# Layer 1's entry in a streaming two-layer decode kernel: ticks on VectorE, a loop entered without the last kept scores, and two early copies

## The chip, the cores and the metric

The kernel runs on one core of one Trainium2 chip. Its time is the device time of one launch in microseconds; three runs of the kernel before were timed, and their median is used. Only a difference of more than about 0.2% (5.1 us) is counted as faster or slower.

## The reference

Two rows `x` (B = 2, D = 576) go twice through an attention block A and a mixer block B, with the same caches and weights both times:

```
x = x + A(layernorm(x)); x = x + B(layernorm(x))      # layer 0
x = x + A(layernorm(x)); x = x + B(layernorm(x))      # layer 1

A: q = x @ wq                      # 32 heads of 128, one query row per batch
   scores = q . k_cache * 128**-0.5 over 16384 keys
   o = softmax(scores) @ v_cache
   return o @ wo
B: h = gelu(layernorm(x) @ w1); shifts of h @ w2 -> hs
   x1 = x + hs
   return x1 + gelu(layernorm(x1) @ w3) @ w4
```

`k_cache` and `v_cache` are (2, 32, 16384, 128) in bf16: 64 pairs of batch and head, 4096 KB of K and 4096 KB of V each. Both layers read all of both, so that nearly all bytes of the run are cache tiles.

## The kernel before

**Tiles and slots.** One K tile or one V tile is 128 partitions x 32768 B (`TILE`). On-chip memory has six slots of that size, numbered 0 to 5, and a small area `AUX` ahead of them, which holds the three buffers `kt[0..2]` for transposed chunks of K. A head's K tile holds 128 blocks of 128 keys; it is treated as two halves of 64 blocks (`BP`). In each half the first 32 blocks (`PB`) go to TensorE and the other 32 to VectorE.

**One head in the loop** (`attention`, the loop over `s`). TensorE takes its blocks in eight chunks of eight blocks (`CH`): `transposes` writes a chunk to a PSUM bank `tps`, `evacuate` copies it on ScalarE to a `kt` buffer (line 1257), and `scores` multiplies it with the query column `q_col` (line 1272) into the bank `sps[s % 3]`. VectorE handles the other blocks in four calls of `dots`, at chunks 0, 2, 4 and 6: a product with the broadcast query `qb` (TENSOR_TENSOR, line 1302) and a sum (TENSOR_REDUCE, line 1306). These four cover blocks 32 to 47, 48 to 63, 96 to 111 and 112 to 127. After the first `dots`' chunk, at `c == LEAD`, VectorE also runs `keep_o(s - 2)` (line 1343: the finished output of an earlier head leaves the PSUM column `ops`), `softmax_max(s - 1)` (lines 1317 and 1319), then the second `dots`, then `q_column(s + 1)` (line 1188). `first_max(s)` (line 1311) closes the head on VectorE. `softmax_exp(s - 1)` on ScalarE and `pv` (line 1362) on TensorE finish the head before. The loop runs over 63 heads, as 21 turns of three, on TensorE, ScalarE and VectorE; the code of GpSimd and SyncE is written out.

**Transfers.** All transfers go through one queue on SyncE, in the order in which they were planned (`Store.plan`). `pump` issues the head of that list as soon as all memory cells of its place have been released in program order; SyncE then waits for the semaphores of the operations that used the place last. Most tiles are one transfer of 4096 KB. Layer 1's first new tiles are cut: the rest of `v61` into three pieces, `k0` into quarters 0, 1, 3, 2 for slot 1, and `k1` into quarters 0, 2, 1, 3 for slot 3. After them come `v0`, `k2`, `v1`, `k3` and so on as whole tiles. Layer 1 takes the heads in the order 63, 61, 62, 0, 1, ...; the K tiles 61 to 63 and the V tiles 62 and 63 are kept from layer 0. So `k0` takes the place of K63 (head s = 0 of layer 1), `k1` that of K61 (s = 1), and `k2` that of K62 (s = 2).

**Signals.** An operation has a target `to`. One with `to="vector"` increments a semaphore that only VectorE waits on; one with `to=None` increments its engine's common semaphore. When another engine has to wait for an operation whose `to` is not that engine, `_stand_in` lets it wait for the next operation of the same engine with `to=None`:

```
x = next(x for x in self.ops[d.eng][d.pos + 1:] if x.to is None and not x.relay)
```

All operations of `dots` have `to="vector"`, `q_column` and `keep_o` have `to="tensor"`. In the loop of the kernel before, the operations of VectorE with `to=None` are the second operation of `softmax_max` (line 1319) and `first_max`. SyncE therefore waits on line 1319 for the first `dots` of a head, and on `first_max` for the second, third and fourth.

**Waits at a loop's entry.** A wait inside a loop has to have the same form in each turn. Where the first turn has a wait that later turns don't have, `_loop` puts it ahead of the loop (`ahead`).

**Layer 1's head s = 0.** Its K tile lies on chip while layer 0 still runs its mixer. `ahead` transposes its chunks early: four chunks stay in the four `tps` banks (`held_over`, "kept chunks"), twelve (`early`) are copied back in place by `lay`. When the query is there, `early_scores` (line 1287) makes the scores of the twelve, VectorE copies part of them (line 1103) and takes `first_max(0)`. Then the four kept chunks are evacuated to `kt` and scored, and the loop begins.

Of the kernel before, what the change touches and what calls it, by code (L numbers as in the profile page):

```python
# [338 lines left out]
class KB:  # L339
# [718 lines left out]
    def attention(self, l):  # L1058
        U, LEAD, NS = self.U, self.LEAD, self.NS
        o = self.order(l)  # L1060
        n = self.PB // self.CH
        pend = []

        def step(s, c):
            self.transposes(l, s, o[s], c)
            pend.append((s, o[s], c, self.chunk))
            self.chunk += 1
            self.evacuate(pend[-1][3])
            if len(pend) > LEAD:
                self.scores(*pend.pop(0))  # L1070

        def rest():
            while pend:
                self.scores(*pend.pop(0))

        if l == 0:
            self.store.claim("kt", 0, self.AUX)
            zero = self.zero[:, 0, 0:1]
            self.pe(lambda pe: pe.matmul(self.mps[:, 448:449], lhsT=self.ident[:, :], rhs=zero, start=True, stop=True,
                                         skip_group_check=True), reads=["ident", "zero"], writes=["ops", "mps"], to="vector").needed = True  # L1080
            self.q_broadcast(0)
            self.landed("k", o[0], True)
            for c in range(2 * n):
                step(0, c)
                if c % n in (0, 2):
                    self.dots(l, 0, o[0], c // n, c % n // 2)
                if c == LEAD:
                    self.q_column(1)
            rest()
            self.q_spread(1)  # L1090
            self.first_max(0)
        else:
            self.lay(0, len(self.laid))
            assert self.made == len(self.early) and len(self.held_over) == self.HOLD
            pend += self.held_over
            self.chunk += len(self.early) + self.HOLD
            w = self.NB - 2 * self.PB
            for i, (h, b, col) in enumerate(self.early):
                self.early_scores(l, o[0], h * self.BP + b, col)
                if i == 1:  # L1100
                    self.q_broadcast(1)
                if i == w // self.CH - 1:
                    self.dv(lambda e: e.tensor_copy(out=self.s_dve[0][:, 0:w], in_=self.mps[:, 2 * self.PB:self.NB]),
                            reads=["mps"], writes=[("s_dve", 0)], to="vector")
                    self.first_max(0)
            self.store.claim("kt", 0, self.AUX)
            for i, x in enumerate(self.held_over):
                if i >= self.NKT:
                    self.scores(*pend.pop(0))
                self.evacuate(x[3])  # L1110
            rest()
        first = self.g.mark()
        for s in range(1, U):
            self.landed("k", o[s], True)
            for c in range(2 * n):
                step(s, c)
                if c == LEAD:
                    self.keep_o(s - 2)
                    self.softmax_max(s - 1)
                if c % n in (0, 2):  # L1120
                    self.dots(l, s, o[s], c // n, c % n // 2)
                if c == LEAD:
                    self.q_column(s + 1)
            self.first_max(s)
            rest()
            self.softmax_exp(s - 1)
            self.q_spread(s + 1)
            self.landed("v", o[s - 1], False)
            for g in range(4):
                self.pv(l, s - 1, o[s - 1], g)  # L1130
        self.g.loop(first, (U - 1) // NS, NS, self.HEAD[l])
        self.touch(ACT.Exp)
        self.ahead(l, self.HOLD)
        self.store.release("kt")
        self.last_head(l, U - 1, o[U - 1])

    def last_head(self, l, s, u):

        U, late = self.U, self.late
        first = next(a + late - v for a, v, n in self.runs(l) if v <= late < v + n)  # L1140
        assert self.order(l)[first] == late and first < s
        i, hg = self.ident[:, :], self.HG
        every = bass.AP(tensor=i.tensor, offset=i.offset, ap=[list(i.ap[0]), [1, hg], [0, hg], [hg, 128 // hg]])
        self.softmax_max(s)
        self.keep_o(s - 1)
        self.dv(lambda e: e.tensor_copy(out=self.every.rearrange("p (j h m) -> p j h m", j=hg, h=hg), in_=every),
                reads=["ident"], writes=["prod", "every"])
        self.shares(0, first)
        self.normed(l, 0, first)
        self.ahead(l, 1)  # L1150
        self.dealt(0, late, self.sps[2], ("sps", 2), self.masked[0], self.oA[:, :], "oA")
        self.lay(l, 1)
        self.ahead(l, 1)
        self.softmax_exp(s)
        self.touch(ACT.Sqrt)
        self.lay(l, 1)
        self.landed("v", u, False)
        for g in range(4):
            self.pv(l, s, u, g)
        self.keep_o(s, None)  # L1160
        n = [sum(c[0] < a for c in self.cuts["wo", l]) for a in (1, 2)] + [len(self.cuts["wo", l])]
        for i in range(n[0]):
            self.heads_projection(l, i)
        self.shares(first, U)
        self.normed(l, first, U)
        for i in range(n[0], n[1]):
            self.heads_projection(l, i)
        self.dealt(late, U, self.sps[0], ("sps", 0), self.masked[1], self.oB[:, :], "oB")
        self.ahead(l, 1)
        self.lay(l, 1)  # L1170
        for i in range(n[1], n[2]):
            self.heads_projection(l, i)
        self.add_rows(self.x, "x", self.sps[1], ("sps", 1))
# [89 lines left out]
        n = self.CH * 256  # L1263
        return self.store.key(k * n, n)

    def scores(self, s, u, c, at):
        k = at % self.NKT
        sp = s % self.NS

        def f(pe):  # L1270
            for j in range(self.CH):
                ins = pe.matmul(self.sps[sp][:, c * self.CH + j:c * self.CH + j + 1], lhsT=self.kt[k][:, j, :],  # L1272
                                rhs=self.q_col[:, sp:sp + 1], start=True, stop=True, skip_group_check=True)
            return ins
        last = c == 2 * self.PB // self.CH - 1
        self.pe(f, reads=[("q_col", sp)] + self.kt_keys(k), writes=[("sps", sp)], sig=("s", c, k, sp),
                to="vector" if last else None)

# [171 lines left out]
```

## Time and profile before

| | |
|---|---|
| median of 3 runs | 2553.53 us (2553.32 to 2553.66) |
| profiled execution, its own time | 2553.28 us |
| its span in the trace | 2551.2 us |
| time outside the span | 2.08 us |
| bytes moved, mean rate over the span | 1093.00 MB, 428 GB/s |
| busy: PE, DVE, ACT, POOL | 1523.6, 1875.7, 1115.2, 164.2 us |

PE is TensorE, DVE is VectorE, ACT is ScalarE, POOL is GpSimd, SP is SyncE; SPq and POOLq are their queues of instructions. All times of the trace count from the span's start. In timelines the columns are start, duration, engine, line, operation, `out<-in`, count, and in brackets the engine's idle time ahead of the row with what ended it. In tables of stretches each engine has its busy time and, in parentheses, its count of instructions; the last three columns are the clock granted to TensorE, the mean busy share of the 16 DMA engines, and the rate in GB/s.

### The profile page before, as it was taken

How to read it: one execution, taken by the hardware profiler on the slowest of the kernel's cores; microseconds unless marked ns; L12 is line 12 of the kernel's file. 1: busy time of each engine (PE TensorE's matmuls, PEld its weight loads, DVE VectorE, ACT ScalarE, POOL GpSimd, SP SyncE). 2: the span in 40 equal slices, each digit the busy share in tenths (PEclk: the TensorE clock that was granted, in tenths of full speed). 3: DMA queues.
4: the chain of work that ended last, by engine and by line, in shares of the span. 5: the costliest groups of instructions: out<-in, count | busy, mean ns of one | idle time of the engine just before them, and what ended most of it. 6: DMA issues, size and time to landing. Idle time of an engine off the chain costs nothing.

```text
span 2551.2 us, 75163 instructions
## 1 busy us (share of the span) xinstructions
PE 1523.6 (60%) x34485; PEld 1435.3 (56%) x34485; DVE 1875.7 (74%) x1794; ACT 1115.2 (44%) x1833; POOL 164.2 (6%) x161
## 2 busy tenths in 40 slices
PE   5555555655565565556677655565565556556556
PEld 4555555555555555555677655555555555555555
DVE  5877776777777677777649877777677777777773
ACT  3444444443444444344355443444344344434442
POOL 0000000000000000000000000000000000000000
PEclk8666666666666666666657666666666666666665
DMA  9999999999999999999999999999999999999999
GB/s 412 428 433 430 433 431 432 432 432 433 431 433 431 433 430 433 430 433 430 422 379 430 430 433 431 433 432 432 432 432 432 431 432 431 433 431 434 430 434 387
DMA packets 46498, 1093.00 MB, mean 428 GB/s; under 512 B 5114, under 2 KB 6780, under 8 KB 11516
## 3 DMA queue, kind: packets, MB, share of 16 engines
q1 hardware_dynamic: 46460, 1092.46, 99.9%
q8 instruction: 28, 0.46, 0.1%
q14 instruction: 10, 0.08, 0.0%
HBM read 1092.44 MB, written 0.00 MB: 428 GB/s over the span
## 4 chain that ended last, share of the span: by engine, by line
DMA 70%; DVE 19%; issue 8%; PE 2%; SPq 0%; ACT 0%; POOLq 0%; DVEq 0%
DMA mem<-in_A_k_cache_dram 64%; DVE prod L1302 9%; DVE s_dve L1306 9%; DMA mem<-in_B_w_dram 2%; DMA mem<-in_A_wo_dram 2%; DMA mem<-in_A_v_cache_dram 2%; PE tps L1242 0%; PE mps L1362 0%; SPq L98 0%; DVE mx L1311 0%; DVE mx L1319 0%; DMA mem<-in_A_wq_dram 0%; DVE q_col L1188 0%; DVE o_acc L1343 0%; DVE mx L1317 0%
## 5 line engine op out<-in xcount | busy, mean ns | idle before, releaser
L1257 ACT ACTIVATE mem<-tps 128x1024 bf16<-128x1024 bf16 x1020 | 958.2, 1035 | 1289.7 <-PE tps L1242 1286.3
L1242 PE MATMUL tps<-ident,mem 128*128 128x128 bf16 x8160 | 813.8, 271 | 708.5 <-POOLq L187 707.9
L1306 DVE TENSOR_REDUCE s_dve<-prod 128x16 f32<-128x2048 bf16 x508 | 1161.4, 2286 | 17.4
L1242 PEld LDWEIGHTS tps<-ident,mem 128*128 128x128 bf16 x8160 | 670.3, 124 | 718.5 <-POOLq L187 717.4
L1302 DVE TENSOR_TENSOR prod<-mem,qb 128x2048 bf16<-128x2048 bf16 x508 | 621.3, 1223 | 541.1 <-POOLq L187 530.4
L1362 PE MATMUL mps<-p,mem 128*128 128x1 bf16 x16384 | 450.4, 165 | 83.3 <-POOLq L187 73.1
L1362 PEld LDWEIGHTS mps<-p,mem 128*128 128x128 bf16 x16384 | 443.0, 102 | 98.2 <-ACT p L1336 97.0
L1272 PE MATMUL sps<-q_col,mem 128*128 128x1 bf16 x8160 | 369.0, 166 | 161.4 <-ACT mem L1257 144.0
L1272 PEld LDWEIGHTS sps<-q_col,mem 128*128 128x128 bf16 x8160 | 320.8, 101 | 217.8 <-ACT mem L1257 211.4
L1322 POOL PARTITION_ALL_REDUCE mx<-mx x128 | 160.3, 1252 | 2334.9 <-DVE mx L1319 2334.9
L1332 ACT ACTIVATE p<-s_dve,mx 128x64 bf16<-128x64 f32 x128 | 44.7, 349 | 15.5
L1201 ACT ACTIVATE qb<-sps 128x128 bf16<-128x128 f32 x129 | 34.1, 264 | 32.7 <-PE sps L1198 32.7
L1198 PE MATMUL sps<-ident,q_col 128*128 128x128 bf16 x129 | 29.8, 231 | 20.2 <-DVE q_col L1188 20.2
L1336 ACT ACTIVATE p<-sps,mx 128x64 bf16<-128x64 f32 x128 | 37.7, 295 | 0.0
L1330 ACT ACTIVATE mx<-mx 128x1 f32<-128x1 f32 x128 | 30.3, 237 | 12.9 <-POOL mx L1322 12.9
L1311 DVE TENSOR_REDUCE mx<-s_dve 128x1 f32<-128x64 f32 x128 | 28.2, 220 | 4.5
L882 PE MATMUL sps<-xn,mem 128*128 128x2 bf16 x544 | 21.4, 173 | 13.8 <-DMA mem<-in_A_wq_dram 7.5
L882 PEld LDWEIGHTS sps<-xn,mem 128*128 128x128 bf16 x544 | 20.0, 119 | 15.3 <-DMA mem<-in_A_wq_dram 8.3
L1317 DVE TENSOR_REDUCE mx<-sps 128x1 f32<-128x64 f32 x128 | 27.4, 214 | 0.7 <-DVEq L259 0.7
L1343 DVE COPY o_acc<-mps 128x1 f32 (+1 forms) x130 | 19.3, 149 | 7.2 <-PE mps L1362 7.2
L1198 PEld LDWEIGHTS sps<-ident,q_col 128*128 128x128 bf16 x129 | 12.6, 98 | 21.1 <-DVE q_col L1188 21.1
L1336 ACT ACTIVATION_READ_ACCUMULATOR p<-sps,mx (+1 forms) x128 | 24.4, 191 | 0.0
(107 smaller groups left out, 228.0 us busy)
## 6 DMA issues: line engine op xcount, KB each, us to landing
mem<-in_A_v_cache_dram SPq DMA_DIRECT2D x125, 4096.0 KB, 45.5
mem<-in_A_k_cache_dram SPq DMA_DIRECT2D x123, 4096.0 KB, 43.2
mem<-in_A_wq_dram SPq DMA_DIRECT2D x8, 1024.0 KB, 11.7
mem<-in_A_k_cache_dram SPq DMA_DIRECT2D x8, 1024.0 KB, 7.5
mem<-in_B_w_dram SPq DMA_DIRECT2D x14, 576.0 KB, 7.2
mem<-in_B_w_dram SPq DMA_DIRECT2D x7, 864.0 KB, 21.3
mem<-in_B_w_dram SPq DMA_DIRECT2D x4, 1152.0 KB, 16.5
mem<-in_A_wo_dram SPq DMA_DIRECT2D x6, 576.0 KB, 8.2
```

Source lines behind the costliest of these rows:

```text
L882: ins = pe.matmul(out[:, m * B:(m + 1) * B], lhsT=buf[:, c:c + 127 * d + 1:d], rhs=self.xn[:, k, :], start=first and m == lo, stop=False, ...
L1198: self.pe(lambda pe: pe.matmul(qps, lhsT=self.wide(self.q_col[:, i:i + 1]), rhs=self.ident[:, :], start=True, stop=True, skip_group_check= ...
L1201: self.act(lambda e: e.activation(out=self.qb[s % self.NS][:, :], in_=qps, func=ACT.Copy), reads=[("qps", i)], writes=[("qb", s % self.NS) ...
L1242: ins = pe.transpose(out[:, j * 128:(j + 1) * 128], buf[:, j * 128:(j + 1) * 128], self.ident[:, :])
L1257: self.act(lambda e: e.activation(out=self.kt[k], in_=self.tps[t][:, :].rearrange("p (i c) -> p i c", i=self.CH), func=ACT.Copy), reads=[( ...
L1272: ins = pe.matmul(self.sps[sp][:, c * self.CH + j:c * self.CH + j + 1], lhsT=self.kt[k][:, j, :], rhs=self.q_col[:, sp:sp + 1], start=True ...
L1302: self.dv(lambda e: e.tensor_tensor(out=prod, in0=buf.rearrange("p (j d) -> p j d", d=128), in1=qbc, op=ALU.mult), reads=[("qb", s % self. ...
L1306: self.dv(lambda e: e.tensor_reduce(out=sd[:, c0:c0 + DB], in_=prod, axis=AX.X, op=ALU.add), reads=["prod"], writes=[("s_dve", s % self.NS ...
L1322: self.pool(lambda e: e.partition_all_reduce(self.mx[:, 3, m:m + 1], self.mx[:, 2, m:m + 1], channels=128, reduce_op=ROP.max), reads=[("mx ...
L1332: self.act(lambda e: e.activation(out=p[:, n:self.NB], in_=self.s_dve[s % self.NS][:, :], func=ACT.Exp, bias=self.mx[:, 4, m:m + 1], scale ...
L1336: self.act(lambda e: e.activation(out=p[:, 0:n], in_=self.sps[i][:, 0:n], func=ACT.Exp, bias=self.mx[:, 4, m:m + 1], scale=self.scale, acc ...
L1362: ins = pe.matmul(self.mps[:, 448:449], lhsT=buf[:, j * 128:(j + 1) * 128], rhs=p[:, col:col + 1], start=(h == 0 and b == 0), stop=(h == 1 ...
```

## The change

Four things change, all in `attention` and `scores`:

- `tick()`: a new one-element copy on VectorE behind `q_column(s + 1)`, in each head of both loops. It has `to=None`, so it becomes the stand-in for the second `dots` of a head.
- In layer 1, the claim of `AUX` moves ahead of the early scores, and two of the four kept chunks are evacuated there, ahead of the query. The third is evacuated behind the second early chunk and `q_broadcast(1)`; the first kept chunk is scored and the fourth evacuated behind the fourth early chunk; the other three are scored behind the twelfth.
- The last kept scores get `to="vector"` (`last=True`).
- The matmul with zeros into the column `ops`, which layer 0 had ahead of its loop, becomes the function `first_o` and is also called ahead of layer 1's loop. It, too, has `to="vector"`.

```
         if l == 0:
             self.store.claim("kt", 0, self.AUX)
-            zero = self.zero[:, 0, 0:1]
-            self.pe(lambda pe: pe.matmul(self.mps[:, 448:449], lhsT=self.ident[:, :], rhs=zero, start=True, stop=True,
-                                         skip_group_check=True), reads=["ident", "zero"], writes=["ops", "mps"], to="vector").needed = True
+            self.first_o()
             self.q_broadcast(0)
...
             self.lay(0, len(self.laid))
             assert self.made == len(self.early) and len(self.held_over) == self.HOLD
-            pend += self.held_over
+            held = self.held_over
             self.chunk += len(self.early) + self.HOLD
+            self.store.claim("kt", 0, self.AUX)
+            for x in held[:2]:
+                self.evacuate(x[3])
             w = self.NB - 2 * self.PB
             for i, (h, b, col) in enumerate(self.early):
                 self.early_scores(l, o[0], h * self.BP + b, col)
                 if i == 1:
                     self.q_broadcast(1)
+                    self.evacuate(held[2][3])
+                if i == 3:
+                    self.scores(*held[0])
+                    self.evacuate(held[3][3])
                 if i == w // self.CH - 1:
                     self.dv(lambda e: e.tensor_copy(out=self.s_dve[0][:, 0:w], in_=self.mps[:, 2 * self.PB:self.NB]),
                             reads=["mps"], writes=[("s_dve", 0)], to="vector")
                     self.first_max(0)
-            self.store.claim("kt", 0, self.AUX)
-            for i, x in enumerate(self.held_over):
-                if i >= self.NKT:
-                    self.scores(*pend.pop(0))
-                self.evacuate(x[3])
-            rest()
+            for x in held[1:]:
+                self.scores(*x, last=x is held[-1])
+            self.first_o()
         first = self.g.mark()
...
                 if c == LEAD:
                     self.q_column(s + 1)
+                    self.tick()
             self.first_max(s)
...
+    def tick(self):
+
+        self.dv(lambda e: e.tensor_copy(out=self.sc[:, 8, 0:1], in_=self.mean_f[:, :]), reads=["mean_f"], writes=["tick"])
+
+    def first_o(self):
+
+        zero = self.zero[:, 0, 0:1]
+        self.pe(lambda pe: pe.matmul(self.mps[:, 448:449], lhsT=self.ident[:, :], rhs=zero, start=True, stop=True,
+                                     skip_group_check=True), reads=["ident", "zero"], writes=["ops", "mps"], to="vector").needed = True
...
-    def scores(self, s, u, c, at):
+    def scores(self, s, u, c, at, last=False):
...
-        last = c == 2 * self.PB // self.CH - 1
+        last = last or c == 2 * self.PB // self.CH - 1
         self.pe(f, reads=[("q_col", sp)] + self.kt_keys(k), writes=[("sps", sp)], sig=("s", c, k, sp),
                 to="vector" if last else None)
```

## The prediction

> **What bounds the kernel now.** I read the page first, then the stretches around the seam between the layers, then the timelines of the engines there.
>
> ```profile
> span 2551.2 us, 75163 instructions
> ...
> DMA  9999999999999999999999999999999999999999
> GB/s 412 428 433 430 433 431 432 432 432 433 431 433 431 433 430 433 430 433 430 422 379 430 430 433 431 433 432 432 432 432 432 431 432 431 433 431 434 430 434 387
> ```
>
> The DMA engines are busy all along, and nearly every slice of 63.8 us moves 430 to 434 GB/s. I take 432 as the full rate; a 4096 KB tile (4.19 MB) then takes 9.7 us, a quarter 2.4. An edit that moves no bytes can only win where the rate sags: the first slice, the slices of 422 and 379 at the seam, and the last. The table in stretches of 5 us shows where the seam loses:
>
> ```profile
> 1325.00:1330.00 5.00, 3.17 (x85) 2.52 (x82) 4.97 (x4) 4.00 (x10) 0.00 (x0) 0.98 1.01 395
> 1330.00:1335.00 5.00, 5.00 (x121) 5.00 (x119) 4.90 (x5) 1.56 (x2) 0.00 (x0) 0.50 0.25 105
> 1335.00:1340.00 5.00, 4.38 (x90) 4.05 (x87) 4.90 (x7) 5.00 (x7) 1.25 (x1) 0.84 0.88 328
> 1340.00:1345.00 5.00, 3.69 (x123) 3.43 (x124) 4.96 (x4) 2.00 (x7) 0.00 (x0) 0.85 1.17 496
> 1345.00:1350.00 5.00, 5.00 (x82) 5.00 (x80) 4.90 (x5) 3.35 (x4) 0.00 (x0) 0.50 0.99 423
> 1350.00:1355.00 5.00, 3.43 (x77) 3.00 (x74) 4.90 (x7) 4.67 (x7) 1.25 (x1) 0.97 0.87 334
> 1355.00:1360.00 5.00, 3.38 (x125) 3.38 (x126) 4.97 (x4) 0.77 (x5) 0.00 (x0) 0.71 0.97 416
> ```
>
> The last column sums to 2497, or 12.5 MB in 35 us; at 432 GB/s they take 28.9 us, so the seam loses 6.1 us here: most in one hole around 1330 to 1336, about 1 us in a second at 1350. VectorE (third column) meanwhile is busy without a pause. What SyncE was waiting for:
>
> ```profile
> 1323.42 0.33 SPq L98 DMA_DIRECT2D mem<-in_A_k_cache_dram  x1
> 1326.62 0.33 SPq L98 DMA_DIRECT2D mem<-in_A_k_cache_dram  x1
> ...
> 1334.52 0.80 SPq L98 DMA_DIRECT2D mem<-in_A_k_cache_dram  x2
> 1335.37 0.43 SPq L98 DMA_DIRECT2D mem<-in_A_v_cache_dram  x1
> ...
> 1349.28 0.33 SPq L98 DMA_DIRECT2D mem<-in_A_k_cache_dram  x1
> 1349.65 0.43 SPq L98 DMA_DIRECT2D mem<-in_A_v_cache_dram  x1
> ```
>
> These are k1's quarters 0 and 2 (released by TensorE), its quarters 1 and 3 together, v0, k2 and v1. Quarters 1 and 3 and k2 wait for VectorE:
>
> ```profile
> 1315.17 0.23 DVE L1103 COPY s_dve<-mps 128x64 f32<-128x64 f32 x1 [1.64 <-PE mps L1287]
> 1315.43 0.22 DVE L1311 TENSOR_REDUCE mx<-s_dve 128x1 f32<-128x64 f32 x1
> 1319.69 1.23 DVE L1302 TENSOR_TENSOR prod<-mem,qb 128x2048 bf16<-128x2048 bf16 x1 [4.04 <-PE sps L1272]
> ...
> 1323.15 0.15 DVE L1343 COPY o_acc<-mps 128x1 f32 x1
> 1323.22 0.21 DVE L1317 TENSOR_REDUCE mx<-sps 128x1 f32<-128x64 f32 x1
> ...
> 1324.79 2.29 DVE L1306 TENSOR_REDUCE s_dve<-prod 128x16 f32<-128x2048 bf16 x1
> 1327.00 0.15 DVE L1188 COPY q_col<-q_f 128x1 bf16 x1
> 1327.12 1.22 DVE L1302 TENSOR_TENSOR prod<-mem,qb 128x2048 bf16<-128x2048 bf16 x1
> 1328.37 2.29 DVE L1306 TENSOR_REDUCE s_dve<-prod 128x16 f32<-128x2048 bf16 x1
> 1330.69 1.22 DVE L1302 TENSOR_TENSOR prod<-mem,qb 128x2048 bf16<-128x2048 bf16 x1
> ...
> 1334.27 0.22 DVE L1311 TENSOR_REDUCE mx<-s_dve 128x1 f32<-128x64 f32 x1
> ...
> 1348.99 0.22 DVE L1311 TENSOR_REDUCE mx<-s_dve 128x1 f32<-128x64 f32 x1
> ```
>
> VectorE is done with `first_max(0)` at 1315.65 and stands still until 1319.69, 4.04 us, held by TensorE's line 1272, the kept scores. From there it runs heads s = 1 and 2 at 14.7 us each (1334.27 to 1348.99). `first_max(1)` ends at 1334.49 and the two quarters go at 1334.52; `first_max(2)` ends at 1349.21 and k2 goes at 1349.28.
>
> **Entering the loop early.** The kept scores and what they wait for:
>
> ```profile
> 1313.91 0.28 ACT L1201 ACTIVATE qb<-sps 128x128 bf16<-128x128 f32 x1 [7.35 <-PE sps L1198]
> 1314.09 2.85 ACT L1257 ACTIVATE mem<-tps 128x1024 bf16<-128x1024 bf16 x3
> 1317.96 1.03 ACT L1257 ACTIVATE mem<-tps 128x1024 bf16<-128x1024 bf16 x1 [1.02 <-PE sps L1272]
> ...
> 1313.67 1.47 PE L1287 MATMUL mps<-q_col,mem 128*128 128x1 bf16 x48
> ...
> 1315.85 0.33 PE L1272 MATMUL sps<-q_col,mem 128*128 128x1 bf16 x7
> 1317.74 0.62 PE L1272 MATMUL sps<-q_col,mem 128*128 128x1 bf16 x17 [1.56 <-issue]
> 1319.04 0.37 PE L1272 MATMUL sps<-q_col,mem 128*128 128x1 bf16 x8 [0.69 <-ACT mem L1257]
> ...
> 1334.90 0.40 PE L1272 MATMUL sps<-q_col,mem 128*128 128x1 bf16 x8
> ```
>
> With its target on VectorE, the last kept scores' signal has the form of every later turn's, so the wait moves from ahead of the loop to `softmax_max(0)`, behind the first `dots`. `first_o` does the same for `keep_o`. The first `dots` needs only `qb(1)` (ready at 1314.19), the tile K61, which is there, and VectorE's turn. That turn is a little later: eight matmuls of the first kept chunk now stand ahead of the copy of line 1103, at 1.47 / 48 = 0.03 us each 0.25 us, so `first_max(0)` ends at 1315.9. To enter the loop VectorE needs between 0.03 us (back to back) and 0.28 us (TensorE's end at 1319.41 to VectorE's start at 1319.69); I take 0.2, as part of that 0.28 may be the signal. The first product starts at 1316.1 instead of 1319.69: 3.6 us earlier (3.5 to 3.75).
>
> It now waits inside the loop, behind the first `dots`, at 1316.1 + 3.46 = 1319.6, with the rest of the head queued behind. TensorE is there in time: the early copies take the two ScalarE pieces of about 1 us off the end, and the 0.69 us wait for the fourth evacuation goes. TensorE's 1.56 us standstill after 104 matmuls (96 early, one broadcast, seven kept) is tied to no wait; I leave it at the same count. Behind it, from 1317.74, are 26 matmuls of 0.03 us, so TensorE is through at 1318.6 instead of 1319.41. Bounds: 1317.1 without the standstill, and 1319.4 if nothing were won. Either is ahead of 1319.6; a doubled standstill would cost VectorE about 0.6 us. TensorE's own chain moves up by 0.8, and k1's quarters 0 and 2 and v0 with it, v0 since it goes on line 1272 of head s = 2 (ended at 1335.30 before, 1334.5 now). The early chunks' quarters of k0 slip by 0.25 to 1.8 us, which the queue covers: the rate holds until 1330, over 10 us on.
>
> **The ticks.** The row of line 1188 shows what a one-element copy costs at this place: between the sum that begins at 1324.79 and the next product at 1327.12 lie 2.33 us, without such a copy (1328.37 to 1330.69) 2.32. So 0.01 us at the least, 0.15 (its busy time) at the most; nothing can be gained, since VectorE runs in order. I take the 0.07 from `keep_o` to the next small operation (1323.15 to 1323.22). The two ticks of heads 1 and 2 take 0.14 us off the lead. What the tick brings: k1's quarter 1 waits for the second `dots` at about 1323.7 instead of `first_max(1)`, and goes right behind quarter 2 at about 1326. Its 2.4 us then fill the first hole's beginning.
>
> **The other ticks**, 124 of them, lie beside transfers:
>
> ```profile
> L1302 DVE TENSOR_TENSOR prod<-mem,qb 128x2048 bf16<-128x2048 bf16 x186 | 227.5, 1223 | 218.7 <-POOLq L187 217.1
> ```
>
> Over 46 heads of layer 1 VectorE waits 217.1 us for tiles to land, 4.7 us a head. A tick costs nothing as long as the head's work stays 4.7 us under its transfers. At the layers' ends tiles are freed with the queue still full, so nothing is counted there. `first_o` is one matmul of 0.03 us.
>
> **The sum, along the transfers.** The old stock runs out at about 1331.2 as before (105 GB/s over 1330 to 1335 are 0.53 MB, 1.2 us at the full rate). Quarter 1 takes it to 1333.6. `first_max(1)` ends 3.5 us earlier, at 1331.0; quarter 3 follows at once. How long until it moves bytes? Before, an issue at 1334.52 gave 328 GB/s over 1335 to 1340, 3.8 us' worth, so it counted from 1336.2, 1.7 us later. So quarter 3 counts from 1333.6 to 1336.0, and v0, issued at 1334.5, from 1336.2 to 1345.9. k2 goes when `first_max(2)` ends, 1349.28 - 3.6 + 0.14 = 1345.8, and counts from 1347.5. Before it counted from 1349.28 + 1.7 = 1351.0 (two quarters and v0 lasted until 1350.8). So the first hole closes, a new one of about 1.6 us opens in front of k2, and everything from k2 on, a continuous stream to the end, moves up by 3.5 us. Of 6.1 us lost, 2.6 remain. Behind k2 each head gives 19.4 us of transfers for 14.7 of VectorE's work, so no third hole opens. The profiled execution's 2553.28 (span 2551.2 plus 2.08) becomes 2549.8; the median lies 0.25 above the profiled time, so the forecast is 2550.0, by its own bounds 2549.4 to 2550.6.
>
> **Rivals.** *The wait stays.* If any other operand of the loop's first turn still holds VectorE until TensorE's kept scores are through, it enters at 1318.6 + 0.28 = 1318.9, and the lead is 0.8 - 0.14 = 0.7: 2552.8. The tick alone then only shifts the hole from before quarter 1 to before k2. For it: the 4.04 us are put down to the releaser that came last, and a second one may stand just behind. Against: the copy, `qb(1)` and K61 are all there by 1316.
>
> *More is won.* If k2 were released by something earlier than `first_max(2)`, up to the whole 6.1 us would come back: 2547.4. Against: k2 is one transfer for a whole tile, and VectorE reads the tile's last blocks just ahead of `first_max(2)`.
>
> *Slower: the ticks are on the path.* If VectorE set the pace of each head, 126 ticks at 0.146 us (line 1188's kind) would cost 18.4 us, less 3.5 won: 2568.4; at 0.07 each, 8.8 - 3.5, 2558.8. The page's chain that ended last and its table of issues bear on it:
>
> ```profile
> DMA 70%; DVE 19%; issue 8%; PE 2%; SPq 0%; ACT 0%; POOLq 0%; DVEq 0%
> ...
> mem<-in_A_k_cache_dram SPq DMA_DIRECT2D x123, 4096.0 KB, 43.2
> ```
>
> For it: VectorE has 19% of that chain. Against: a K tile takes 43.2 us from issue to landing where 9.7 would do, so tiles queue at the transfers and not at VectorE; the rival decides only from 19.4 us of work a head, and there are 14.7. [...]
>
> **How the numbers follow.** The forecast has 0.72, the wait that stays 0.12, more won 0.08, slower 0.08. A difference of 0.2% is 5.1 us, about what a measurement of this kernel can tell from no change; 3.5 us is 0.14%. So same has 0.72 + 0.12 = 0.84, faster 0.08, slower 0.08. The range holds the forecast with 0.4 us more on its fast side, and the wait that stays: 2549.0 to 2553.2, which leaves out 0.16.
>
> **What would show it.** In the changed profile the first product of layer 1 (line 1302) should start near 1316.1 with next to no idle time; `first_max(1)` near 1330.8 and `first_max(2)` near 1345.6; one quarter of k1 should go near 1326, another near 1331. The stretch 1330 to 1335 should be near full rate, and a smaller dip should stand at 1346 to 1348. I am wrong if VectorE still shows a wait for line 1272 ahead of the loop, if it stops behind the first `dots` for TensorE, or if heads in the steady part no longer wait for line 187.

## The result: 2550.47 us, a good 3 us less

| | median | lowest to highest | runs | ratio to before, 95% interval |
|---|---|---|---|---|
| before | 2553.74 | 2552.93 to 2555.32 | 22 | |
| changed | 2550.47 | 2548.54 to 2552.22 | 22 | 0.9986 [0.998, 0.9992] |

In two further sets of runs the changed kernel had medians of 2549.92 and 2549.50 us (11 runs each) beside 2553.78 and 2553.73 before. So it is 3.3 to 4.2 us faster, clear of no difference, yet under 0.2%. The forecast was 2550.0.

The page of the changed kernel, the same lines as were shown of before:

```profile
span 2549.0 us, 75293 instructions
...
DMA  9999999999999999999999999999999999999999
GB/s 413 427 435 429 435 429 435 429 434 430 433 431 431 432 431 433 430 433 430 423 403 424 431 433 431 432 432 431 432 431 433 430 433 430 433 430 433 430 433 381
```

The clear change is in the slices at the seam: 422, 379 and 430 became 423, 403 and 424. In this profiled run layer 0 happened to end 1.2 us later. Times at the seam are therefore compared below as times **behind the query**, the start of the cast that makes layer 1's first `q_col` (line 910): 1312.86 before, 1314.07 here. VectorE's timeline, first of before and then of the changed kernel (start, duration, engine, line, operation):

```profile
1312.86 0.16 DVE L910 CAST q_col<-sps 128x1 bf16<-128x1 f32 x1 [8.92 <-PE sps L882]
```

```profile
1314.07 0.16 DVE L910 CAST q_col<-sps 128x1 bf16<-128x1 f32 x1 [8.93 <-PE sps L882]
...
1316.60 0.23 DVE L1108 COPY s_dve<-mps 128x64 f32<-128x64 f32 x1 [1.85 <-PE mps L1300]
1316.86 0.22 DVE L1324 TENSOR_REDUCE mx<-s_dve 128x1 f32<-128x64 f32 x1
1317.10 1.22 DVE L1315 TENSOR_TENSOR prod<-mem,qb 128x2048 bf16<-128x2048 bf16 x1
...
1322.21 2.29 DVE L1319 TENSOR_REDUCE s_dve<-prod 128x16 f32<-128x2048 bf16 x1
1324.41 0.15 DVE L1201 COPY q_col<-q_f 128x1 bf16 x1
1324.47 0.14 DVE L1142 COPY sc<-mean_f 128x1 f32<-128x1 f32 x1
1324.53 1.22 DVE L1315 TENSOR_TENSOR prod<-mem,qb 128x2048 bf16<-128x2048 bf16 x1
...
1331.68 0.22 DVE L1324 TENSOR_REDUCE mx<-s_dve 128x1 f32<-128x64 f32 x1
...
1346.40 0.22 DVE L1324 TENSOR_REDUCE mx<-s_dve 128x1 f32<-128x64 f32 x1
```

The 4.04 us of standstill ahead of the first product are gone: it starts 0.02 us behind `first_max(0)`, 3.03 us behind the query instead of 6.83. The lead of 3.80 us is still whole at `first_max(2)`, 32.33 us behind the query instead of 36.13. SyncE's issues of the changed kernel (start, duration of issuing, destination and source, count):

```profile
1323.76 0.33 SPq L98 DMA_DIRECT2D mem<-in_A_k_cache_dram  x1
...
1327.02 0.80 SPq L98 DMA_DIRECT2D mem<-in_A_k_cache_dram  x2
...
1331.93 0.33 SPq L98 DMA_DIRECT2D mem<-in_A_k_cache_dram  x1
...
1335.78 0.33 SPq L98 DMA_DIRECT2D mem<-in_A_v_cache_dram  x1
...
1346.70 0.33 SPq L98 DMA_DIRECT2D mem<-in_A_k_cache_dram  x1
```

k1's quarter 1 now goes together with quarter 2 (1327.02), quarter 3 alone behind `first_max(1)`, and k2 at 1346.70, 32.63 us behind the query instead of 36.42. The stretches of 5 us (the last column is the rate):

```profile
1325.00:1330.00 5.00, 3.42 (x86) 3.03 (x84) 4.90 (x4) 4.40 (x10) 0.00 (x0) 0.84 1.01 408
1330.00:1335.00 5.00, 5.00 (x133) 5.00 (x131) 4.93 (x4) 1.11 (x2) 0.00 (x0) 0.50 1.03 403
1335.00:1340.00 5.00, 5.00 (x90) 5.00 (x88) 4.93 (x9) 4.91 (x6) 1.25 (x1) 0.62 1.03 413
1340.00:1345.00 5.00, 3.38 (x115) 3.06 (x113) 4.90 (x4) 2.64 (x8) 0.00 (x0) 0.72 1.01 429
1345.00:1350.00 5.00, 5.00 (x102) 5.00 (x99) 4.93 (x5) 2.86 (x4) 0.00 (x0) 0.60 0.97 377
1350.00:1355.00 5.00, 3.58 (x77) 2.78 (x74) 4.93 (x9) 4.88 (x7) 1.25 (x1) 1.00 0.98 413
1355.00:1360.00 5.00, 4.26 (x136) 4.12 (x136) 4.90 (x4) 0.68 (x5) 0.00 (x0) 0.59 1.02 436
```

The hole of 105 and 328 GB/s is gone; a dip to 377 is left in front of k2. The seven rates sum to 2879, where before they summed to 2497. Reckoned as in the prediction (35 us less sum x 5 / 432), these 35 us lose 1.7 us instead of 6.1. This **loss at the seam** is one measure of the experiments below, beside their medians. It counts packets in fixed stretches, so it has a scatter of its own: 1.4 to 1.7 us in three profiles of the changed kernel.

A second measure is the tiles themselves. From some 128 us behind the query on, VectorE waits once in each head for its K tile to land. The products behind the second of these waits and behind the last, first of before and then of the changed kernel:

```profile
1460.96 1.23 DVE L1302 TENSOR_TENSOR prod<-mem,qb 128x2048 bf16<-128x2048 bf16 x1 [4.63 <-POOLq L187]
...
2490.56 1.23 DVE L1302 TENSOR_TENSOR prod<-mem,qb 128x2048 bf16<-128x2048 bf16 x1 [4.63 <-POOLq L187]
```

```profile
1458.81 1.22 DVE L1315 TENSOR_TENSOR prod<-mem,qb 128x2048 bf16<-128x2048 bf16 x1 [4.62 <-POOLq L187]
...
2488.38 1.23 DVE L1315 TENSOR_TENSOR prod<-mem,qb 128x2048 bf16<-128x2048 bf16 x1 [4.61 <-POOLq L187]
```

That is 148.10 and 1177.70 us behind the query before, and 144.74 and 1174.31 here: the tiles land 3.4 us earlier, at both ends of the stream. This **lead of the tiles** is 1.0 us less than the fall of the loss at the seam, 6.1 - 1.7 = 4.4.

### The profile page after: what moved, and what is told of

The parts are those of the page before. It is cut to its first block, busy times and chain, and to the rows that moved or that the text cites. A ratio compares the mean times of both kernels' runs of the same rounds, so it can differ in the third digit from the quotient of the medians.

```text
span 2549.0 us, 75293 instructions
## 1 busy us (share of the span) xinstructions
PE 1523.7 (60%) x34486; PEld 1434.2 (56%) x34486; DVE 1875.6 (74%) x1920; ACT 1114.2 (44%) x1833; POOL 164.1 (6%) x161
## 4 chain that ended last, share of the span: by engine, by line
DMA 70%; DVE 20%; issue 8%; PE 1%; SPq 0%; POOLq 0%; DVEq 0%; ACT 0%
DMA mem<-in_A_k_cache_dram 64%; DVE s_dve L1319 9%; DVE prod L1315 9%; DMA mem<-in_B_w_dram 2%; DMA mem<-in_A_wo_dram 2%; DMA mem<-in_A_v_cache_dram 1%; DVE mx L1324 0%; SPq L98 0%; DVE mx L1332 0%; DMA mem<-in_A_wq_dram 0%; DVE q_col L1201 0%; DVE o_acc L1356 0%; DVE mx L1330 0%; PE tps L1255 0%; PE sps L882 0%
## 5 line engine op out<-in xcount | busy, mean ns | idle before, releaser
L1345 ACT ACTIVATION_READ_ACCUMULATOR p<-s_dve,mx (+1 forms) x128 | 23.8, 186 | 0.0
```

Of the source, the lines that this page charges most:

```text
L1345: self.act(lambda e: e.activation(out=p[:, n:self.NB], in_=self.s_dve[s % self.NS][:, :], func=ACT.Exp, bias=self.mx[:, 4, m:m + 1], scale ...
```

## The experiments

The theory: k2's issue waits for `first_max(2)`, and VectorE's earlier entry moves that. Two rivals: the ticks carry the gain, as they fill the first hole; or the early copies do, as they free TensorE. Each run stands beside the kernel before of its own set (2553.88 in the first four, 2553.78 in the next four, 2553.73 in the last three).

| run | first product behind the query | k2's issue behind the query | loss at the seam | lead of the tiles, second wait and last | median of 11 | to before, ratio interval |
|---|---|---|---|---|---|---|
| before | 6.83 | 36.42 | 6.1 | | | |
| changed (first profile) | 3.03 | 32.63 | 1.7 | 3.4, 3.4 | 2550.47 (22 runs) | -3.3, [0.998, 0.9992] |
| entry, no ticks | 3.03 | 32.63 | 2.2 | 3.7, 3.2 | 2550.81 | -3.1, [0.9979, 0.9998] |
| ticks alone | 6.98 | 36.58 | 5.3 | 0.5, 0.5 | 2552.65 | -1.2, [0.9987, 1.0005] |
| late copies | 2.82 | 32.78 | 2.5 | 2.5, 2.4 | 2551.33 | -2.6, [0.9981, 0.9999] |
| wait kept | 6.17 | 35.77 | 4.6 | 1.4, 1.3 | 2551.84 | -2.0, [0.9983, 1.0001] |
| changed, second set | 3.03 | 32.62 | 1.4 | 3.5, 3.5 | 2549.92 | -3.9, [0.9977, 0.9995] |
| twelve ticks | 3.03 | 33.93 | 2.8 | 3.1, 3.1 | 2550.13 | -3.7, [0.9977, 0.9995] |
| k2 cut | 3.03 | in quarters | 1.2 | 4.5, 3.8 | 2549.45 | -4.3, [0.9973, 0.9991] |
| k2 cut, no ticks | 3.03 | in quarters | 2.5 | 3.3, 3.3 | 2550.87 | -2.9, [0.9979, 0.9997] |
| k2 cut, third set | 3.04 | in quarters | 0.8 | 5.1, 5.0 | 2549.26 | -4.5, [0.9975, 0.9993] |
| v0 and k2 cut | 3.04 | in quarters | 0.8 | 4.9, 4.7 | 2548.91 | -4.8, [0.9973, 0.9991] |
| changed, third set | 3.04 | 32.64 | 1.5 | 4.3, 4.1 | 2549.50 | -4.2, [0.9974, 0.9992] |

In the nine profiles with k2 in one piece, the tile of the second wait lands 111.0 to 112.8 us behind k2's issue, while the issue itself lies anywhere from 32.6 to 36.6 us behind the query. So the stream follows k2's issue, as the theory has it. The three profiles of the changed kernel have k2's issue at the same distance and differ by 0.9 us in the lead of the tiles, so a difference of less than about 1 us between two single profiles shows nothing by itself. In two runs (entry without ticks, k2 cut in the second set) the stream lost 0.6 us at one head in the middle of layer 1; why isn't known.

**The entry without the ticks.**

```
                 if c == LEAD:
                     self.q_column(s + 1)
-                    self.tick()
```

> The changed kernel without its ticks. Theory (VectorE's earlier entry carries the gain, since k2 waits for first_max(2)): the first product of layer 1 still starts about 3.0 us behind the query (the cast of q_col) instead of 6.8, and first_max(2) about 32.3 us behind it; quarter 1 of k1 goes with quarter 3 at first_max(1), so that a hole of about 1.8 us comes back ahead of it and the one in front of k2 goes; the time is that of the changed kernel, 2550.5 us (2550.0 to 2551.1). Rival (the ticks carry it by filling the first hole): the gain is gone, 2553.7 us.

Median 2550.81. SyncE's issues and the stretch with the hole:

```profile
1330.84 2.29 SPq L98 DMA_DIRECT2D mem<-in_A_k_cache_dram  x2
```

```profile
1330.00:1335.00 5.00, 5.00 (x101) 5.00 (x99) 4.90 (x8) 2.47 (x3) 0.26 (x1) 0.50 0.85 305
```

Quarters 1 and 3 go together again, at `first_max(1)`, and a hole is back in that stretch (305 GB/s, 1.5 us' worth). Most of the gain stays: the loss is 2.2 us, the tiles land 3.7 and later 3.2 us earlier, and k2 goes at the same distance from the query. The rival in which the ticks carry the gain has fallen.

**The ticks alone**: the kernel before, with the line left out above and the function `tick` added.

> The kernel before with the ticks alone. Theory: quarter 1 of k1 goes right behind quarter 2, but first_max(2) stands where it stood, 36.1 us behind the query, so the hole only moves from in front of quarter 1 to in front of k2; 2553.7 us (2553.2 to 2554.2). Rival (the ticks carry the gain): 2550.5 to 2551 us. Rival (ticks are on the path in each head): 2559 us or more.

Median 2552.65, between the theory's 2553.7 and the rival's 2551, and outside the range given; its interval still holds no difference. VectorE's entry and k2's issue:

```profile
1320.07 1.23 DVE L1307 TENSOR_TENSOR prod<-mem,qb 128x2048 bf16<-128x2048 bf16 x1 [4.19 <-PE sps L1277]
```

```profile
1349.67 0.33 SPq L98 DMA_DIRECT2D mem<-in_A_k_cache_dram  x1
```

The query of this run was at 1313.09, so VectorE still stands still until 6.98 us behind it, and k2 goes at 36.58, 0.16 us *later* than before. Yet the loss falls from 6.1 to 5.3 us, and the tiles land 0.5 us earlier. One reading is that in the kernel before k2 did not start to move when its issue allowed it, since the two quarters and v0 ahead of it took up to 0.8 us longer than that, and that the ticks take this away. A gain of 0.5 to 0.8 us in a single profile doesn't show it; what the ticks alone cannot be is the whole gain.

**The late copies**: all evacuations of kept chunks go back behind the early scores, while the signal to VectorE and `first_o` stay.

```
-            for x in held[:2]:
-                self.evacuate(x[3])
...
+            for x in held[:3]:
+                self.evacuate(x[3])
+            self.scores(*held[0])
+            self.evacuate(held[3][3])
             for x in held[1:]:
                 self.scores(*x, last=x is held[-1])
             self.first_o()
```

> The changed kernel with all four kept chunks evacuated behind the early scores, in the old order, but with the signal to VectorE and first_o. Theory: VectorE enters the loop about 0.2 us earlier still than in the changed kernel and then stops behind its first dots for TensorE, which is through at about 6.5 us behind the query as before, so 0.3 to 0.6 us are lost; 2550.9 us (2550.3 to 2551.5). Rival (TensorE's and ScalarE's earlier copies carry the gain): 2552.9 us or more.

Median 2551.33, in the theory's range. VectorE enters at 2.82 us and stops behind its first `dots`, for `first_o`:

```profile
1319.93 0.16 DVE L1354 COPY o_acc<-mps 128x1 f32 x1 [0.27 <-PE mps L1145]
```

It stands only 0.27 us, and k2 goes 0.15 us later than in the changed kernel. The loss is 0.8 us higher (2.5), more than that: v0, which waits for TensorE, goes 22.29 us behind the query instead of 21.71. Whether v0 makes up all the rest wasn't tried. The early copies are worth 0.8 us by these losses and 0.8 to 1.8 us by the lead of the tiles: about a microsecond.

**The wait kept**: early copies and ticks stay, `last=` and `first_o` of layer 1 go.

```
             for x in held[1:]:
-                self.scores(*x, last=x is held[-1])
-            self.first_o()
+                self.scores(*x)
```

> The changed kernel with the early copies and the ticks, but without the last kept scores' signal to VectorE and without first_o, so that the wait stands ahead of the loop as before. Theory: VectorE enters with TensorE's end, about 5.8 to 6.0 us behind the query instead of 3.0, a lead of 0.8 to 1.0 us over the kernel before; 2552.9 us (2552.4 to 2553.4). Rival (the earlier copies carry the gain): 2550.5 us.

```profile
1319.20 1.23 DVE L1314 TENSOR_TENSOR prod<-mem,qb 128x2048 bf16<-128x2048 bf16 x1 [3.17 <-PE sps L1284]
```

With the query at 1313.03 this is 6.17 us behind it: VectorE waits for the kept scores again, 3.17 us, and enters a bit later than the 5.8 to 6.0 expected. k2 goes at 35.77, 0.65 us earlier than before. The median, 2551.84, lies below the range of 2552.4 to 2553.4. The loss of 4.6 accounts for 1.5 us and the lead of the tiles for 1.4: the 0.65 of k2, and perhaps up to 0.8 from the ticks, which the theory had at nothing. The other half microsecond of the 2.0 is within the scatter. The rival, in which the copies carry the gain, asked for 2550.5 and has fallen.

**Twelve ticks in place of one** (the copies go to twelve elements of `x6`, which is free during the loops).

```
-                    self.tick()
+                    for i in range(12):
+                        self.tick(i)
```

> The changed kernel with twelve one-element copies at the place of each tick. Theory (a tick costs only its step on VectorE, and only in heads 1 and 2 of layer 1 does that count): eleven more at about 0.06 us are 0.66 us a head, 1.3 us by first_max(2); 2551.8 us (2551.2 to 2552.5). Rival (ticks are paid in each head): 126 x 0.66 = 83 us more, about 2634 us.

VectorE at that place, and its group of products over 1500 to 2400 us, here and then in the changed kernel (busy, mean ns, idle time ahead and its releaser):

```profile
1321.50 2.29 DVE L1320 TENSOR_REDUCE s_dve<-prod 128x16 f32<-128x2048 bf16 x1
1323.70 0.15 DVE L1202 COPY q_col<-q_f 128x1 bf16 x1
1323.77 0.81 DVE L1143 COPY x<-mean_f 128x1 f32<-128x1 f32 x12
1324.49 1.22 DVE L1316 TENSOR_TENSOR prod<-mem,qb 128x2048 bf16<-128x2048 bf16 x1
```

```profile
L1316 DVE TENSOR_TENSOR prod<-mem,qb 128x2048 bf16<-128x2048 bf16 x186 | 226.9, 1220 | 183.9 <-POOLq L187 182.3
```

```profile
L1315 DVE TENSOR_TENSOR prod<-mem,qb 128x2048 bf16<-128x2048 bf16 x186 | 227.3, 1222 | 214.1 <-POOLq L187 212.5
```

From the sum's start to the next product lie 2.99 us instead of 2.32: eleven more copies cost 0.67, 0.061 us each. In the steady part VectorE pays them from its idle time, 182.3 us instead of 212.5, so the rival at 2634 us is far off. At the seam k2 goes 1.3 us later, as expected, and the loss is 1.4 us higher than the changed kernel's in the same set. The median rose by only 0.2 us, to 2550.13, below the range of 2551.2 to 2552.5. The tiles land 3.1 us earlier than before, where the changed kernel of this set has 3.5, so they too moved by less than the loss says. A shift of 1.3 us is hard to see in any case beside the scatter of the changed kernel's runs (3.5 us).

**k2 in quarters.** The planned cuts of layer 1's first tiles get one more, so that k2 need not wait for `first_max(2)` as a whole:

```
+            if i == 4:
+                cuts = [(q * j, q) for j in (0, 2, 1, 3)]
```

> The changed kernel with k2 cut into quarters 0, 2, 1, 3, as k1 is. Theory (the hole left is the one in front of k2, and only because the whole tile waits for first_max(2)): its quarters 0 and 2 go when TensorE is through with them and quarter 1 at head 2's tick, while v0 is still moving, so the hole of about 1.6 us closes and the time falls to 2548.9 us (2548.3 to 2549.7). Rival (something else is next late, v0's release by TensorE or a later tile): 2550.5 us.

Median 2549.45, in the theory's range; the loss is 1.2 us, and the tiles land 4.5 and later 3.8 us earlier.

> The same without ticks. Theory: the hole in front of k1's quarter 1 (about 1.8 us) comes back and is now no longer covered by k2's wait, so the ticks are worth 1.3 to 1.8 us here: 2550.4 us (2549.8 to 2551.0). Rival (the ticks do nothing in this kernel at all): as with ticks, 2548.9 us.

The same without ticks had 2550.87, 1.4 us above it in the same set, and its loss is 1.3 us higher. This was the forecast: once most of k2 isn't held by `first_max(2)`, the hole ahead of k1's quarter 1 is no longer covered by anything, and the ticks are worth more than in the changed kernel.

> The changed kernel with k2 in quarters, again, beside the changed kernel in the same set. Theory: the stream of transfers from k2 on runs about 0.5 us further ahead than in the changed kernel (counted from the query), so the median is 0.3 to 0.8 us lower than that of the changed kernel in this set. Rival (the difference of the last set was scatter): no lower.

The third set: 2549.26, beside 2549.50 for the changed kernel. That is 0.24 us lower, less than the 0.3 to 0.8 expected; whether this version is the faster one can't be told from these runs.

> The changed kernel as the measure of this set: 2550.2 us (2549.5 to 2551.2); the first product 3.03 us and first_max(2) 32.33 us behind the query, as in its other profiles.

> The changed kernel again, on the chip of the other runs of this set, as their measure: 2550.5 us (2549.5 to 2551.2).

The changed kernel's two sets kept to these distances from the query. Their medians, 2549.50 and 2549.92, lie in the ranges given, 0.6 to 0.7 us below the values expected; the first of them is at its range's lower end.

**v0 in quarters as well** (`if i == 3: cuts = [(q * j, q) for j in range(4)]`).

> k2 and v0 both in quarters. In the changed kernel v0 goes at 21.6 us behind the query, on TensorE's scores of head 2, while its place is read block by block from about 15.5 us on. Theory (a rest of the loss at 20 to 26 us behind the query is v0's late release): its first quarters go right behind k1's last at about 18.2 us, the rate there rises from some 370 to over 400 GB/s, and 0.3 to 0.6 us are won on the version with k2 alone in quarters. Rival (the rate there is that of quarters, whose packets are 8 KB, not of a late release): nothing won, or up to 0.5 us lost, as v0 now moves in quarters too.

```profile
1330.00:1335.00 5.00, 5.00 (x103) 5.00 (x100) 4.90 (x8) 2.41 (x3) 0.16 (x1) 0.50 1.00 388
...
1345.00:1350.00 5.00, 5.00 (x68) 5.00 (x66) 4.90 (x8) 4.28 (x5) 0.45 (x1) 0.50 1.01 418
```

v0's first quarters do go early (18.24 us behind the query), but 1330 to 1335 moves 388 GB/s, no more than the changed kernel's 403: that part of the theory is wrong, the late release wasn't what kept the rate down there. The rival, that this is the rate of quarters, isn't tested apart from it. The dip in front of k2 is gone (418 where it was 377), the loss is 0.8 us, as with k2 alone cut. The median is 0.35 us below that of k2 alone cut in the same set, a gain in the theory's range; as neither the rate nor the loss moved, it can't be put down to the theory's mechanism. The median of 2548.91 is the lowest of all and its runs are the closest (2548.67 to 2549.79), 0.6 us under the changed kernel in the same set. Against the kernel before this is clear; against the changed kernel, whose runs reach from 2548.54 to 2551.18, it is not.

## Why the prediction was right

**The entry.** Forecast 3.24 us behind the query, measured 3.03. The term chosen too high was the step into the loop: 0.02 us instead of 0.2, so the back-to-back end of the bounds. The eight matmuls put ahead of line 1103's copy cost 0.22 us (2.31 to 2.53 us behind the query; forecast 0.25).

**TensorE in time.** Its timeline in the changed kernel:

```profile
1316.42 0.97 PE L1300 MATMUL sps<-q_col,mem 128*128 128x1 bf16 x31
1319.02 0.19 PE L1300 MATMUL sps<-q_col,mem 128*128 128x1 bf16 x1 [1.64 <-issue]
1319.07 0.78 PE L1285 MATMUL sps<-q_col,mem 128*128 128x1 bf16 x24
1319.71 0.17 PE L1147 MATMUL mps<-zero,ident 128*128 128x1 bf16 x1
```

The standstill is there, 1.64 us, in front of the last early matmul, behind 104 matmuls (one broadcast, eight kept, 95 early), at the same count as before. TensorE is through 5.81 us behind the query (forecast 5.74), before VectorE gets to `keep_o` at 6.50, and VectorE doesn't stop. The late copies show the other side of that margin.

**The ticks' cost.** 2.32 us from the sum to the next product, as between two operations with no copy at all: nothing, where 0.01 had been the lower bound and 0.07 was taken. Only further ticks behind the first cost time, 0.061 us apiece in the row of twelve.

**The sum.** Its mechanism held: the first hole closed, a dip opened in front of k2, no third one came. Its outcome held too: it moves everything from k2 on up by 3.5 us, and the tiles land 3.4, 3.5 and 4.1 to 4.3 us earlier in the three profiles of the changed kernel. Its terms were less exact. The lead at k2's issue is 3.8 us, not 3.46, by the two points above. The dip left in front of k2 is (432 - 377) x 5 / 432 = 0.6 us, and 0.9 and 1.0 in the other two profiles, not 1.6. By the loss at the seam 4.4 to 4.7 us came back, not 3.5; by that measure the step "two quarters and v0 lasted until 1350.8" was too short, and the ticks, which the sum had at no gain of their own, were worth up to 0.8 us. The tiles don't bear this out: with the ticks left out they land 3.7 us earlier at the second wait, within the 3.4 to 4.3 of the changed kernel. Why the two measures differ, the runs don't settle.

**What came back at the end.** The medians show 3.3 to 4.2 us, about the lead of the tiles. From the query to the end of the span lie 1238.3 us before, and 1234.9, 1236.3 and 1234.3 in the profiles of the changed kernel (spans 2549.0, 2549.1 and 2546.8). From the last wait for a K tile to the end of the span it is 60.6 us before, and 60.6, 62.2 and 60.7, so only the second of them lost part of its lead at the end. There TensorE waited longer for the last weights; its waits from 2515 us to the end, first before, then in that run (total, times, longest, us):

```profile
PE sps L956 <- DMA mem<-in_A_wo_dram: 0.6, 2, 0.4
```

```profile
PE sps L956 <- DMA mem<-in_A_wo_dram: 2.8, 3, 1.6
```

That is 2.2 us more in one run, and may be part of why the changed kernel's runs scatter over 3.7 us and those before over 2.4. Whether a stream that is further ahead meets such a delay more often, or whether it is chance, the runs don't settle. That the forecast, 2550.0, came within 0.5 us of all three medians is in part luck: the changed kernel's own medians lie 1.0 us apart, and the two terms that were off, the lead and the dip, would both have raised the gain above 3.5 us, which the tiles show in one of three profiles only.

**The rivals.** The wait that stays is what *wait kept* shows, and the changed kernel doesn't have it. *More is won* fell as well: k2 still goes only when `first_max(2)` has ended (1346.62, issue at 1346.70). VectorE as the bound of each head is excluded by the twelve ticks: over 46 heads they leave it 182.3 us of waits for tiles.

## What to carry to other kernels

In a kernel whose transfers never rest, list the transfers around each dip in the rate with what each of them waits for, and follow the last one: a wait removed ahead of an earlier transfer only counts as far as the later one moves too. Here the ticks alone, with k2 at 36.58 us behind the query, brought the tiles forward by 0.5 us; the entry without the ticks, with k2 at 32.63, by 3.2 to 3.7. Check what the rate near the dip says against the landing of tiles far behind it: here the two differed by up to 1.2 us. A wait that a loop's first turn has and the later turns don't have is paid ahead of the whole loop (4.04 us here); giving it the later turns' form puts it behind work that doesn't need it (the first product moved from 6.83 to 3.03 us behind the query). When two bounds come out within a few tenths of a microsecond of each other, as 1350.8 and 1351.0 did here, price the change under both, since the cheap edit that moves only one of them may be worth nothing or most of a microsecond: the ticks alone gained 0.5 us by the tiles and 0.8 by the loss.

## What was not expected of the hardware

A one-element copy on VectorE behind another, behind a sum of 2.29 us, added no time to the start of the next product (2.32 us with and without it), while twelve in a row added 0.061 us for each after the first. TensorE's standstill without a wait stayed at the same count of matmuls, 104, when the order of the work around it was changed, at 1.56 us before and 1.64 here (1.48 to 1.76 in the first four experiments).
